# Polysketch attention in front of a SwiGLU block: late batches' queries sketched with tokens on the partitions, their denominators and turning on VectorE, numerators in 16 tiles, and the first batch reordered

## The chip, the cores and the metric

One core of one Trainium2 chip. The metric is the device time of one execution in microseconds. All runs were in the fast state (granted TensorE clock 0.995 to 1.00). Every ratio below is the mean time of one kernel's fast runs over that of the kernel before in the same rounds on the same chip, so it is not quite the ratio of the medians that stand beside it.

## The reference, cut to what matters

```python
# 4 batches, 4 heads, 1088 tokens, head size 32, sketch size r = 8
def phi(x):                                   # 64 features of a token and head
    a = einsum('rd,bhsd->bhsr', S1, x)
    b = einsum('rd,bhsd->bhsr', S2, x)
    return einsum('bhsi,bhsj->bhsij', a, b).reshape(..., r * r)
q_p, k_p = phi(q), phi(k)
kv  = einsum('bhsf,bhsd->bhfd', k_p, v)
z   = sum(k_p, axis=2)
num = einsum('bhsf,bhfd->bhsd', q_p, kv)
den = einsum('bhsf,bhf->bhs', q_p, z)[..., None] + 1e-06
x   = (num / den), heads side by side         # 4352 tokens x 128
out = (silu(x @ w_gate) * (x @ w_val)) @ w_out   # d_ff = 1536
```

The feed-forward part is most of the arithmetic: 12 blocks of tokens (384, 384 and 320 columns in each batch), 12 chunks of d_ff, three matmuls each, so 432 full-array fp32 matmuls. The weights, S1 and S2 come as 64-bit doubles and are converted on the chip; q, k and v come as fp32.

## The kernel before: the parts concerned

A *unit* is one block and one chunk: two matmuls, Silu on ScalarE, the product on VectorE. A third matmul ("down") follows. Attention for batch b+1 is a generator, advanced between units of batch b, so its work on the other engines hides behind feed-forward matmuls, and its own matmuls are *inserted* between them.

```python
def unit(i, j, late=False):
    g, u = bank(), bank()
    for o, w in ((g, wg), (u, wv)):
        nc.tensor.matmul(o[:, 0:n], w[:, j, :], xT[:, t0 : t0 + n], ...)
    nc.scalar.activation(sg, g, AF.Silu)
    nc.vector.tensor_tensor(out=hj, in0=sg, in1=u, op=ALU.mult)     # some go to GpSimd, "late"

def narrow(dst, raw, shape):          # a weight piece, 64-bit to fp32, in three stages
    nc.vector.tensor_scalar(e, hi, 0x7FF00000, ...)                 # 1: exponent, mantissa
    nc.vector.tensor_scalar(m, hi, 0xFFFFF, 0x100000, ...)
    yield
    nc.scalar.activation(e, e, AF.Relu, ...)                        # 2
    nc.scalar.activation(f, m, AF.Copy, scale=2.0**-20)
    yield
    nc.vector.scalar_tensor_tensor(out=e, in0=hi, scalar=-(1 << 31), in1=e, ...)   # 3: the sign
    nc.vector.scalar_tensor_tensor(out=f, in0=lo, scalar=2.0**-52, in1=f, ...)     #    the low word
    mul = nc.vector if first else nc.gpsimd
    mul.tensor_tensor(out=dst, in0=f, in1=e.bitcast(FP32), op=ALU.mult)
    ...

def attention(b, prods=None):         # a late batch (cut)
    ... key sketches and features on VectorE, their sums zs on GpSimd
    key_values(kvp[:, 0, :], phk, 0, NC)                   # 36 matmuls, 128*32
    for h in range(H):
        nc.tensor.matmul(kvp[32*h : 32*h+32, 1, 0:F], ones[:], zs[:, h, :], ...)
    ... turn_kv: kv and z turned and replicated by matmuls with the identity
    for i, (x0, n) in enumerate(steps):                    # three query steps
        phq = query_features(n, query_products(x0, n, tags))   # features on the partitions
        yield
        nd = totals(n, phq, kvz, ...)       # numerators AND denominators, 16 matmuls of 64*32
        divide(b, x0, n, nd)                # turn den, 1/den, turn back, num * (1/den) into xT
        yield
```

The start handles the first batch with nothing to hide behind: warm-up matmuls, sketches, key values, numerators and denominators, then `keep_warm(3, ...)` (three 512-column bf16 matmuls that compute nothing), `divide` and the first unit.

Of the kernel before, what the change touches and what calls it, by code (L numbers as in the profile page):

```python
# [1 line left out]

# [10 lines left out]
ALU = mybir.AluOpType  # L13
PSUM = bass.MemoryType.PSUM
# [3 lines left out]
def kernel(  # L18
# [37 lines left out]
    F = R * R  # L56
# [49 lines left out]
    qld = const.tile([P, NX, Dh], FP32, name="qld")  # L106
    vld = const.tile([P, H, NC, Dh], FP32, name="vld")
    kT = const.tile([P, NC, 4, 32], FP32, name="kT")
    qT = const.tile([P, HX, 2, 32], FP32, name="qT")
# [27 lines left out]
    def load_next():  # L137
        if not coming:
            return
        name, i = coming.pop(0)  # L140
        dst, src = weights[name]
        c0, c1 = pieces[name][i]
        if name == "wo":
            part = src.rearrange("(c p) d -> p c d", p=P)[:, c0:c1, :]
        else:
            part = src.rearrange("p (c f) -> p c f", f=P)[:, c0:c1, :]
        if not wide_w:
            nc.sync.dma_start(out=dst[:, c0:c1, :], in_=part)
            return
        t = raw[name, i] = stage.tile([P, 3, P], I64, tag="raw", name="raw", bufs=NRAW)  # L150
        nc.sync.dma_start(out=t[:, 0 : c1 - c0, :], in_=part)
# [4 lines left out]
    nc.gpsimd.memset(kld[:, NX : 4 * NC, :], 0.0)  # L156
    nc.gpsimd.memset(vld[96:128, :, NC - 2 : NC, :], 0.0)
    load_k(0)
    load_q(0, 0, 2 * XS)
    for i in range(NRAW if wide_w else len(coming)):  # L160
        if i == 2:
            load_v(0, [nc.sync] * 4)
            load_q(0, 2 * XS, 4 * XS)
        load_next()
    load_q(0, 4 * XS, NX)
# [5 lines left out]
    ones = const.tile([P, Dh], FP32, name="ones")  # L171
# [29 lines left out]
    def narrow(dst, raw, shape):  # L201






        words = raw.bitcast(I32)
        pat = "p (n w) -> p n w" if len(shape) == 2 else "p c (n w) -> p c n w"
        words = words.rearrange(pat, w=2)  # L210
        lo = words[..., 0].bitcast(U32)
        hi = words[..., 1]
        first = len(shape) == 2
        tag = "s" if first else ""
        e, m = (
            stage.tile(shape, I32, tag=n + tag, name=n, bufs=6) for n in ("exp", "man")
        )
        f = m[:].bitcast(FP32)
        nc.vector.tensor_scalar(e[:], hi, 0x7FF00000, None, op0=ALU.bitwise_and)  # L219
        nc.vector.tensor_scalar(  # L220
            m[:], hi, 0xFFFFF, 0x100000, op0=ALU.bitwise_and, op1=ALU.bitwise_or
        )
        yield
        nc.scalar.activation(e[:], e[:], AF.Relu, bias=rebias[: shape[0], :], scale=8.0)  # L224
        nc.scalar.activation(f, m[:], AF.Copy, scale=2.0**-20)
        yield
        nc.vector.scalar_tensor_tensor(  # L227
            out=e[:], in0=hi, scalar=-(1 << 31), in1=e[:],
            op0=ALU.bitwise_and, op1=ALU.bitwise_or,
        )  # L230
        nc.vector.scalar_tensor_tensor(  # L231
            out=f, in0=lo, scalar=2.0**-52, in1=f, op0=ALU.mult, op1=ALU.add
        )
        mul = nc.vector if first else nc.gpsimd
        mul.tensor_tensor(out=dst, in0=f, in1=e[:].bitcast(FP32), op=ALU.mult)  # L235
        if not first:
            load_next()
        yield
# [26 lines left out]
    def turn_q(x0, n):  # L265
        nc.vector.transpose(
            out=qT[:, x0 : x0 + n, :, :].rearrange("p x a t -> p (x a) t"),
            in_=qld[:, 2 * x0 : 2 * x0 + 2 * n, :],
        )

    def key_products(ps, c0, c1):

        for c in range(c0, c1):
            for a in (0, 2):
                nc.tensor.matmul(  # L275
                    ps[32 * a : 32 * a + 64, 64 * (c - c0) : 64 * (c - c0) + 64],
                    kT[:, c, a : a + 2, :].rearrange("p a t -> p (a t)"),
# [39 lines left out]
    def unit_sums(kz, phk, c0, c1):  # L317

        for c in range(c0, c1):
# [3 lines left out]
                ones[:],  # L323
# [5 lines left out]
    def turn_kv(kvs, kzp):  # L329

        for half in range(2):
            nc.tensor.matmul(  # L332
                kzp[F * half : F * half + F, 0:P], kvs, ident[:], start=True, stop=True
            )

    def query_products(x0, n, tags):
# [3 lines left out]
        for pr in range(2):  # L340
# [8 lines left out]
            for t in range(2):  # L349
                for half in range(2):  # L350
                    for g in range(2):
# [4 lines left out]
                            qT[r, x0 : x0 + n, half, :],  # L356
# [39 lines left out]
    def totals(n, phq, kvz, nd):  # L396

        w = 32 * n
        for t in (1, 0):
# [16 lines left out]
    def divide(b, x0, n, nd, among=()):  # L416
# [10 lines left out]
        )  # L427
        nc.vector.tensor_scalar_add(rc[:, 0 : 2 * n], dT[:, 0 : 2 * n, 0], 1e-6)
# [4 lines left out]
        if among:  # L433
            part(*among)
# [13 lines left out]
        for x, num, r in todo:  # L448
            nc.vector.tensor_tensor(out=x, in0=num, in1=r, op=ALU.mult)

    def feature_sums(phk):
# [8 lines left out]
        return s[:, 0, :].rearrange("p (h f) -> p h f", h=H)  # L460

    def next_keys(tag):

        both = wide(tag)
        for i, c in enumerate(kpieces):
            key_products(both[:, i, :], *c)
        return [key_copy(both[:, i, :], *c) for i, c in enumerate(kpieces)]

    def attention(b, prods=None):


        if prods is None:
            for c in kpieces:
                turn_k(*c)
                yield
            load_k(b + 1)
            prods = next_keys("b")
        phk = apool.tile([P, NC, H, R, R], FP32, tag="phk", name="phk")
        key_features(phk, prods[0], *kpieces[0])
        yield  # L480
        key_features(phk, prods[1], *kpieces[1])
        zs = feature_sums(phk)
        yield
        kvp = wide("a")
        key_values(kvp[:, 0, :], phk, 0, NC)
        for h in range(H):
            nc.tensor.matmul(
                kvp[32 * h : 32 * h + 32, 1, 0:F], ones[:], zs[:, h, :], start=True, stop=True
            )
        kvs = apool.tile([P, 2, F], FP32, tag="kvs", name="kvs")  # L490
        nc.scalar.copy(kvs[:], kvp[:, :, 0:F])
        if b + 1 < B:
            load_v(b + 1, [nc.sync] * 4)
        turn_q(*steps[0])
        yield
        kvz = apool.tile([P, 2, P], FP32, tag="kvz", name="kvz", bufs=2)
        kzp = bank()[:, 0 : 2 * P].rearrange("p (t n) -> p t n", t=2)
        for t in range(2):
            turn_kv(kvs[:, t, :], kzp[:, t, :])
        nc.scalar.copy(kvz[:], kzp)  # L500
        kvz = kvz[:, 0, :], kvz[:, 1, :]
        tags = "ab"
        for i, (x0, n) in enumerate(steps):
            phq = query_features(n, query_products(x0, n, tags))
            if i + 1 < len(steps):
                turn_q(*steps[i + 1])
            elif b + 1 < B:
                load_q(b + 1)
                turn_k(*kpieces[1])
                if b + 2 < B:  # L510
                    load_k(b + 2)
            yield
            nd = totals(n, phq, kvz, side_by_side(tags[0]))
            last = i + 1 == len(steps)
            if last and b + 1 < B:
                prods = next_keys(tags[1])
            divide(b, x0, n, nd)
            if i == 1 and b + 1 < B:
                turn_k(*kpieces[0])
            tags = tags[::-1]  # L520
            if last:
                return prods
            yield

# [84 lines left out]
    keep_warm(18, 64)  # L609
# [6 lines left out]
    s32 = sraw  # L616
    if wide_s:
        s32 = const.tile([2 * R, Dh], FP32, name="s32")
        run(narrow(s32[:], sraw[:], [2 * R, Dh]))
# [9 lines left out]
    keep_warm(3, ps=bank("acc"))  # L629
# [31 lines left out]
    kvs, zs = (apool.tile([P, F], FP32, name=x) for x in ("kvs0", "zs0"))  # L661
    kvz = [apool.tile([P, P], FP32, name=x) for x in ("kvz0", "kvz1")]
    qbs.append(query_copy(n, *pss[1]))
    nc.scalar.copy(zq[:], kz)
    part("wg", 0)
    key_values(kv, phk, *fpieces[0])
    key_values(kv, phk, *fpieces[1])
    phq = query_features(n, pss, qbs)
    zp = bank("g2")
    for h in range(H):  # L670
        nc.tensor.matmul(
            zp[32 * h : 32 * h + 32, 0:F], sel[:], zq[:, F * h : F * h + F],
            start=True, stop=True,
        )
    key_values(kv, phk, *fpieces[2])
    nc.vector.tensor_copy(zs[:], zp[:, 0:F])
    turn_q(*steps[1])
    for t, s, to, tag in ((1, zs, None, "g0"), (0, kvs, kv, "g1")):
        if to is not None:
            nc.vector.tensor_copy(s[:], to)  # L680
        ps = bank(tag)
        turn_kv(s[:], ps)
        nc.scalar.copy(kvz[t][:], ps[:, 0:P])
    part("wv", 0)
    part("wg", 0)
    nd = totals(n, phq, kvz, ([bank(t) for t in ("g2", "acc")], side_by_side("a")[0]))
# [4 lines left out]
    divide(0, *steps[0], nd, among=("wv", 0))  # L691
# [3 lines left out]
    att = attention(1)  # L695
# [12 lines left out]
    turn_q(*steps[2])  # L708
    unit(0, 2, late=True)
    part("wg", 2)  # L710
# [8 lines left out]
    for _ in range(2):  # L719
# [12 lines left out]
    for z, p in enumerate(both(3, *w) + both(4, *w) + [("wo", i) for i in range(4)]):  # L732
        z += z // 2 * 3
        for at in (z, z + 1, z + 2):
# [5 lines left out]
    groups = (17, 19, 21, 23, 27, 29)  # L740
    for z, (i, j) in enumerate(seq):
# [5 lines left out]
        if z in (16, 24, 25, 26):  # L747
# [9 lines left out]
        if z in groups:  # L757
            next(att)
    todo.sort()
    keys = None  # L760

    def attend():

        nonlocal att, keys
        try:
            if att:
                next(att)
        except StopIteration as end:
            att, keys = None, end.value

    while todo:
# [3 lines left out]
        attend()  # L775
    while att:
        attend()
# [3 lines left out]
    groups = (0, 1, 6, 9, 12, 15, 18, 21, 24)  # L781
    for b in range(1, B):
        att = attention(b + 1, keys) if b + 1 < B else None
        for z in range(3 * NCH):
# [5 lines left out]
            if z in groups:  # L790
                attend()
        while att:
            attend()
# [42 lines left out]
```

## Time and profile before

| | before |
|---|---|
| median of three runs | 321.68 us (321.27 to 321.79) |
| profiled span | 320.2 us, clock 1.00 |
| first feed-forward matmul | 16.70 us |
| 432 feed-forward matmuls at pace | 263.3 us (0.645 us each at 384 columns, 0.538 at 320) |
| inserts and waits of TensorE | 35.8 us: 5.9 up to 52 us (first batch), 29.9 after it (batches 1 to 3) |
| tail | 4.4 us |

This is a ledger: the four parts add to the span. It is read from the timeline of TensorE: the distance between the starts of two neighbouring feed-forward matmuls, less the pace, is what the work or the wait between them costs. Busy time would mislead here, because small matmuls overlap. Starts are measured, while ends are modelled. The lines themselves stand in the prediction.

Where VectorE matters is better seen in busy times by stretch. The columns are the stretch, its length, busy microseconds (and instructions) of PE, PEld, DVE, ACT and POOL, the clock, the DMA share and GB/s. The kernel before:

```profile
17.00:40.00 23.00, 21.45 (x155) 12.09 (x154) 19.71 (x51) 15.74 (x38) 7.80 (x8) 1.00 0.46 131
40.00:60.00 20.00, 19.75 (x65) 11.66 (x63) 17.72 (x37) 10.45 (x23) 7.09 (x7) 1.00 0.47 139
```

On average over the kernel VectorE has half its time free.

### The profile page before, as it was taken

The page shows a single profiled execution, that of the slowest core. Times are in us where ns is not written, and L with a number is a line of the kernel's source. Part 1 is how long each engine was busy: PE and PEld are TensorE (multiplying, and loading weights), DVE is VectorE, ACT ScalarE, POOL GpSimd, SP SyncE. Part 2 cuts the span into 40 slices and gives each one's busy share as a digit, 9 for nine tenths or more (in the row PEclk, how much of TensorE's full clock was granted, in tenths as well). Part 3 has the DMA queues.
Part 4 walks back from the last instruction along what each step waited for, and adds up shares of the span by engine and source line. Part 5 has one row for each costly group of instructions (what it writes and reads, how often), then busy time and mean ns, then how long its engine had stood idle before and what let it go on. Part 6 is the DMA issues. An engine that isn't in the chain of part 4 may idle for free.

```text
span 320.2 us, 5609 instructions
## 1 busy us (share of the span) xinstructions
PE 311.3 (97%) x2300; PEld 193.8 (61%) x2300; DVE 156.5 (49%) x332; ACT 98.6 (31%) x227; POOL 37.7 (12%) x53
## 2 busy tenths in 40 slices
PE   8979999999999999999999999999999999999994
PEld 6545565666566555555676665555667655676664
DVE  4797999543674433555522623535443332323321
ACT  3457765222112223223222223131322222222230
POOL 2224234163000600000000410000000000000000
PEclk9999999999999999999999999999999999999999
DMA  7553490204025020120010100010010100100101
GB/s 201 160 151 100 127 279 0 72 0 97 2 35 151 0 72 2 25 73 0 5 22 0 22 2 3 6 20 0 2 25 0 21 0 2 26 0 0 21 2 25
DMA packets 24665, 13.99 MB, mean 44 GB/s; under 512 B 18368, under 2 KB 22720, under 8 KB 24640
## 3 DMA queue, kind: packets, MB, share of 16 engines
q1 hardware_dynamic: 24000, 13.54, 16.6%
q8 instruction: 18, 0.29, 0.4%
q10 hardware_dynamic: 640, 0.10, 0.2%
q14 instruction: 7, 0.06, 0.1%
HBM read 11.41 MB, written 2.23 MB: 43 GB/s over the span
## 4 chain that ended last, share of the span: by engine, by line
PE 87%; DVE 8%; issue 2%; ACT 1%; POOL 0%; DVEq 0%
PE bank L539 48%; PE bank L567 27%; DVE hj L553 2%; PE a L403 2%; PE a L353 2%; PE bank L197 1%; PE b L353 1%; PE b L275 1%; PE a L309 1%; DVE exp L227 1%; PE a L581 1%; DVE man L231 1%; PE b L403 1%; PE bank L332 1%; DVE exp L219 1%
## 5 line engine op out<-in xcount | busy, mean ns | idle before, releaser
L553 DVE TENSOR_TENSOR hj<-sg,bank 128x384 f32<-128x384 f32 (+1 forms) x138 | 72.5, 527 | 119.7 <-PE bank L539 118.9
L545 ACT ACTIVATE sg<-bank 128x384 f32<-128x384 f32 (+1 forms) x144 | 67.9, 471 | 163.9 <-PE bank L539 162.9
L539 PE MATMUL bank<-xT,wg 128*128 128x384 f32 (+1 forms) x288 | 113.4, 476 | 1.7 <-POOL wg L235 1.1
L539 PE MATMUL bank<-xT,wv 128*128 128x384 f32 (+1 forms) x288 | 111.6, 469 | 0.5 <-DVE hj L553 0.5
L567 PE MATMUL bank<-hj,wo 128*128 128x384 f32 (+2 forms) x288 | 106.9, 463 | 0.4 <-DVE hj L553 0.2
L539 PEld LDWEIGHTS bank<-xT,wv 128*128 128x128 f32 x288 | 54.5, 190 | 34.4 <-DVE hj L553 2.1
L567 PEld LDWEIGHTS bank<-hj,wo 128*128 128x128 f32 x288 | 53.8, 190 | 34.0 <-issue 1.9
L539 PEld LDWEIGHTS bank<-xT,wg 128*128 128x128 f32 x288 | 53.1, 190 | 32.7 <-issue 3.3
L455 POOL TENSOR_TENSOR zs<-phk 128x1024 f32<-128x1024 f32 x3 | 7.0, 2350 | 109.4 <-DVE phk L298 109.4
L381 DVE TENSOR_TENSOR phq<-a,qb 128x384 f32<-128x384 f32 (+1 forms) x11 | 5.8, 527 | 9.2 <-ACT qb L367 9.2
L353 PE MATMUL b<-qT,sq 32*64 32x192 f32 (+1 forms) x176 | 9.3, 324 | 0.0
L353 PE MATMUL a<-qT,sq 32*64 32x192 f32 (+1 forms) x176 | 9.2, 324 | 0.0
L224 ACT ACTIVATE exp<-exp,rebias 128x384 int32<-128x384 int32 (+3 forms) x15 | 8.2, 550 | 3.0 <-DVE exp L219 2.3
L595 DVE STREAM_TRANSPOSE o<-bank 128x384 f32<-128x384 f32 (+2 forms) x12 | 6.5, 543 | 5.4 <-PE bank L567 5.2
L227 DVE SCALAR_TENSOR_TENSOR exp<-raw,exp 128x384 int32<-128x384 int32 (+2 forms) x14 | 8.6, 618 | 0.9 <-ACT exp L224 0.9
L298 DVE TENSOR_TENSOR phk<-ka,b 128x1280 f32<-128x1280 f32 (+1 forms) x6 | 8.1, 1342 | 1.7 <-ACT ka L292 1.7
L367 ACT COPY qb<-a 128x384 f32<-128x384 f32 (+1 forms) x11 | 5.1, 460 | 11.2 <-PE a L353 5.2
L367 ACT COPY qb<-b 128x384 f32<-128x384 f32 (+1 forms) x11 | 5.1, 463 | 9.5 <-PE b L353 6.1
L424 DVE STREAM_TRANSPOSE dT<-a 128x384 f32<-128x384 f32 (+1 forms) x8 | 4.4, 550 | 7.4 <-PE a L403 7.4
L381 DVE TENSOR_TENSOR phq<-b,qb 128x384 f32<-128x384 f32 (+1 forms) x11 | 5.8, 525 | 3.9 <-ACT qb L367 3.9
L353 PEld LDWEIGHTS a<-qT,sq 32*64 32x64 f32 x176 | 5.5, 131 | 3.0 <-PE bank L539 1.6
L231 DVE SCALAR_TENSOR_TENSOR man<-raw,man 128x384 f32<-128x384 uint32 (+2 forms) x14 | 6.9, 492 | 0.0
(90 smaller groups left out, 166.4 us busy)
## 6 DMA issues: line engine op xcount, KB each, us to landing
kld<-in_k_dram SPq DMA_DIRECT2D x4, 544.0 KB, 5.0
vld<-in_v_dram SPq DMA_DIRECT2D x12, 144.0 KB, 4.3
qld<-in_q_dram SPq DMA_DIRECT2D x3, 544.0 KB, 4.4
raw<-in_moe_w_out_dram SPq DMA_DIRECT2D x4, 384.0 KB, 4.7
out_dram<-o SPq DMA_DIRECT2D x28, 48.0 KB, 1.8
raw<-in_moe_w_gate_dram SPq DMA_DIRECT2D x3, 384.0 KB, 3.2
raw<-in_moe_w_val_dram SPq DMA_DIRECT2D x3, 384.0 KB, 3.2
out_dram<-o SPq DMA_DIRECT2D x16, 40.0 KB, 1.7
```

Source lines behind the costliest of these rows:

```text
L224: nc.scalar.activation(e[:], e[:], AF.Relu, bias=rebias[: shape[0], :], scale=8.0)
L227: nc.vector.scalar_tensor_tensor(out=e[:], in0=hi, scalar=-(1 << 31), in1=e[:], op0=ALU.bitwise_and, op1=ALU.bitwise_or,)
L231: nc.vector.scalar_tensor_tensor(out=f, in0=lo, scalar=2.0**-52, in1=f, op0=ALU.mult, op1=ALU.add)
L298: engine.tensor_tensor(out=phk[:, c0:c1, :, :, :].rearrange("p c h i j -> p (c h) i j"), in0=ka.unsqueeze(3).to_broadcast([P, n, R, R]), i ...
L353: nc.tensor.matmul(parts[g][F * half : F * half + F, t, 0:w], sq[r, t, :, :].rearrange("p i j -> p (i j)"), qT[r, x0 : x0 + n, half, :], s ...
L367: nc.scalar.copy(qb[:, :, 0:w], both[:, :, 1, 0:w])
L381: nc.vector.tensor_tensor(out=phq[:, 2 * pr : 2 * pr + 2, 0:w], in0=both[:, :, 0, 0:w], in1=qb[:, :, 0:w], op=ALU.mult,)
L403: nc.tensor.matmul(halves(nd[t])[half][32 * h : 32 * h + 32, 0:w], kvz[t][r, 32 * h : 32 * h + 32], phq[r, h, 0:w], start=True, stop=True,)
L539: nc.tensor.matmul(o[:, 0:n], w[:, j, :], xT[:, t0 : t0 + n], start=True, stop=True)
L545: nc.scalar.activation(sg[:, 0:n], g[:, 0:n], AF.Silu)
L553: nc.vector.tensor_tensor(out=hj[:, 0:n], in0=sg[:, 0:n], in1=u[:, 0:n], op=ALU.mult)
L567: nc.tensor.matmul(acc[i][:, 0:n], wo[:, j, :], hidden[i, j][:, 0:n], start=(j == 0), stop=(j == NCH - 1),)
```

## The change

Its intent: take small matmuls off TensorE, the bound engine, and let VectorE do that work where it has time; and shorten the chain of latencies before the first unit. The diff cut to its core:

```diff
 def attention(b, qsteps):
+    # queries turned and sketched exactly like the keys, tokens on the partitions
+    for ps, src in ((kp, kT), (qp, qT[:].rearrange(...))):
+        for i, c in enumerate(kpieces):
+            key_products(ps[:, i, :], *c, src=src)
...
-    for h in range(H):
-        nc.tensor.matmul(kvp[32*h : 32*h+32, 1, 0:F], ones[:], zs[:, h, :], ...)
+    nc.tensor.matmul(kvz[:, 1, 0 : H * F], ones[:], zs, ...)      # one 128-wide sum
...
-    turn_kv ...
-    for i, (x0, n) in enumerate(steps):
-        phq = query_features(n, query_products(x0, n, tags))
-        nd = totals(n, phq, kvz, side_by_side(tags[0]))
-        divide(b, x0, n, nd)
+    kv turned by two 128*128 matmuls with the identity
+    for s0, s1 in qsteps:                     # batch 1: two steps; later: one
+        for c0, c1 in thirds:
+            nc.vector.tensor_tensor(out=prod, in0=zrep[...], in1=fac[...], op=ALU.mult)
+            yield
+            nc.vector.tensor_reduce(
+                out=dot[:, x, :],
+                in_=phq[:, c0:c1, :, :, :].rearrange("p c h i j -> p (c h) j i"),
+                axis=AX.X, op=ALU.add)
+            yield
+        dot *= b of the query; den = sum of dot + 1e-6; 1/den; a of the query *= 1/den
+        for c0, c1 in thirds:
+            key_features(phq, ...); yield     # features, already divided
+            nc.vector.transpose(out=phT[...], in_=phq[...]); yield
+        for g in range(2):
+            for h in range(H):
+                for a in range(4):            # 16 tiles of 32*32: row a, column h
+                    nc.tensor.matmul(num[a // 2][32*h : 32*h+32, a % 2, 0 : 32 * n],
+                        kvr[32*a : 32*a+32, g, 32*h : 32*h+32], phT[32*a : 32*a+32, h, g, s0 : s0+n, :],
+                        start=(g == 0), stop=(g == 1))
+        copies to xT, half on ScalarE, half on VectorE
...
 # the conversion of a weight piece of two chunks
-    mul.tensor_tensor(out=dst, in0=f, in1=p2, op=ALU.mult)                  # GpSimd
+    first half on VectorE, second half on GpSimd
...
 # the start
-    keep_warm(18, 64)
+    keep_warm(9, 64)
-    keep_warm(3, ps=bank("acc"))             # 512 columns each, after the sketch matrices
+    keep_warm(2, ps=ps); keep_warm(16, 32, ps=ps)
     first weight pieces loaded later and through ScalarE's queue, values before them
-    sums of features: selected by a matmul, copied, turned by matmuls, copied
+    turn_sums(zq, sel[:], ps)                 # turned directly, one copy
+    totals(n, phq, kvz, nd, which=(1,))       # denominators before the numerators
     divide: conversion steps of the second weight pieces moved between its operations
 # one operation of attention per unit where it was one group in every second or third
```

## The prediction

> **What bounds the kernel now.** I read the page first (engine shares, then the chain of waits), then the timeline of the TensorE alone, then the groups by shape for durations, and at the end the timeline of all engines for the first 40 us.
>
> ```profile
> PE 311.3 (97%) x2300; PEld 193.8 (61%) x2300; DVE 156.5 (49%) x332; ACT 98.6 (31%) x227; POOL 37.7 (12%) x53
> PE   8979999999999999999999999999999999999994
> DVE  4797999543674433555522623535443332323321
> PE 87%; DVE 8%; issue 2%; ACT 1%; POOL 0%; DVEq 0%
> ```
>
> TensorE is the bound: 97% busy, 87% of the chain that ended last. VectorE is full only in slices 4 to 6 (24 to 48 us, where the weights are converted). So I count the time as a TensorE ledger: what each piece of work pushes the next feed-forward matmul back by. One feed-forward matmul (two passes, "x2") comes every 0.645 us at 384 columns and every 0.538 us at 320; that is 0.84 ns a column and pass. In the timeline of batch 2 the attention pieces stand between such matmuls:
>
> ```profile
> 133.57 0.81 PE L567 MATMUL bank<-hj,wo 128*128 128x384 f32 x2
> 134.31 0.39 PE L353 MATMUL b<-qT,sq 32*64 32x192 f32 x4
> ...
> 135.17 0.91 PE L539 MATMUL bank<-xT,wg 128*128 128x384 f32 x2
> 135.92 0.81 PE L539 MATMUL bank<-xT,wv 128*128 128x384 f32 x2
> ...
> 140.43 0.81 PE L567 MATMUL bank<-hj,wo 128*128 128x384 f32 x2
> 141.17 0.88 PE L403 MATMUL b<-phq,kvz 64*32 64x192 f32 x32
> 141.98 0.91 PE L539 MATMUL bank<-xT,wg 128*128 128x384 f32 x2
> ...
> 187.10 0.81 PE L567 MATMUL bank<-hj,wo 128*128 128x384 f32 x2
> 187.83 1.21 PE L309 MATMUL a<-phk,vld 128*32 128x64 f32 x72
> 188.86 0.29 PE L487 MATMUL a<-zs,ones 128*32 128x64 f32 x8
> 189.09 0.91 PE L539 MATMUL bank<-xT,wg 128*128 128x384 f32 x2
> ```
>
> The reader sees that an insert costs start to start minus 0.645, plus 0.11 because the matmul behind it takes 0.75 instead of 0.645. Query sketches (32 passes): 135.17-133.57-0.645+0.11 = 1.06 us, and 0.96 at 160 columns. Numerators with denominators (L403): 1.01, 1.01 and 0.90. Key values with feature sums: 1.46, of which the 8 sum passes are 0.22. The same reading gives 1.40 for key sketches alone (36 passes, 59.34 to 61.27) and 1.21 where they follow L403, and 0.60 for turning kv (L332).
>
> The ledger of all gaps: first feed-forward matmul at 16.7; 432 of them at pace, 36 x (8 x 0.645 + 4 x 0.538) = 263.2; inserts and waits 35.8, of which 5.9 in the first batch and 29.9 in batches 1 to 3 (11.8, 9.5, 8.7; the first has about 1.2 of waits); tail 4.4. Sum 320.1, against a span of 320.2. The feed-forward and the tail are not touched; the prize is in 29.9, 5.9 and 16.7.
>
> The start, from the timeline of all engines:
>
> ```profile
> 13.98 0.58 DVE L424 STREAM_TRANSPOSE dT<-a 128x384 f32<-128x384 f32 x1 [0.69 <-PE a L403]
> 16.10 0.46 POOL L235 TENSOR_TENSOR wv<-man,exp 128x128 f32<-128x128 f32 x1 [2.27 <-DVE man L231]
> 16.70 0.88 PE L539 MATMUL bank<-xT,wg 128*128 128x384 f32 x2 [0.58 <-POOL wv L235]
> 20.33 0.91 PE L539 MATMUL bank<-xT,wg 128*128 128x384 f32 x2 [1.08 <-POOL wg L235]
> ```
>
> The first batch is one chain of latencies; TensorE waits in it, once 1.08 us for GpSimd's multiply of a weight piece.
>
> **What the Trainium skill says.** (1) "TensorE: Matmul & The Clock Gate", Part 3, Measured speedup vs the span model: small matmuls on separate 32-row and 32-column tiles run side by side, 16 of them at 10.6 times. The trace agrees for 8 tiles: 32 passes of 192 columns one by one would be 32 x 0.161 = 5.2 us; L403 costs 1.01. No run yet shows 16 tiles. (2) "TensorEngine Tiling (Array Packing)", Key Properties and Gotcha 1: changing the mode drains the engine, and row tiles need different PSUM banks. The first fits the 0.37 us that L403 costs above 4 rounds x 0.161; the new numerators put each row tile in its own bank. (3) "VectorE: DVE Perf Modes", the perf-mode tier table: fp32 tensor_tensor and tensor_reduce run at one element a cycle. The trace: tensor_tensor 936 ns at 768 elements, 1481 at 1280, so 1.06 ns an element plus 0.12 us. No reduce is in the trace; I take it like a tensor_tensor of the elements it reads.
>
> **The change part by part.** TensorE, a late batch with one query step:
> - Removed: three query sketches, 1.06 + 1.06 + 0.96 = 3.08; three numerator and denominator groups, 2.92; the feature replication kv turn, 0.60. The old key sketches (1.2 to 1.4) and key values with sums (1.46) come back changed. Together about 9.3, which with waits is the 29.9 / 3.
> - Keys and queries sketched alike, tokens on partitions: 72 passes, 1.40 + 1.21 = 2.61.
> - Key values 1.46 - 0.22, plus one 128-wide sum of 256 columns in two passes, 2 x 256 x 0.84 ns = 0.43: 1.67.
> - kv turned by two 128-column full-array matmuls: 4 x 0.108 = 0.43, say 0.5.
> - Numerators: 64 passes on 16 tiles, so 4 rounds of 288 (half of them 256) columns: 4 x 0.242 = 0.97, plus 0.37 as at L403: 1.34. Key values issue 72 passes in 1.03, 14 ns each, so 64 need at least 0.92: issue does not forbid it.
> - Sum 6.1. Batch 1 has two query steps; two small groups bounded by issue at 1.1 each make it 7.0. Three batches: 19.2.
>
> VectorE, a late batch. Before: key and query turns 3.2, key features 2.7, query features 3.2, turning and inverting denominators 4.6, final product 1.6: 15.3 us. After: turns of keys and queries 3.1; key features 2.9; products with z 3 x 0.94 and three reduces like them, 5.6; the denominator group of five small operations about 1.7; query features 2.8; their turning 3 x 0.97 = 2.9 (a 640-element turn takes 0.84); half of the final copies 0.7. Sum 19.7, 4.4 more. Between 177 and 250 us VectorE is busy 31.9 of 73.0; it would be 36 of about 70. It is not the bound on average. In detail: one attention operation per unit, at most 0.97 (1.7 for the denominator group) beside a 0.55 product, in a unit of 1.93 us (1.61 at 320 columns). A unit's second bank is wanted again 2.6 us after it is full and the product needs 0.8 of that, so a lump of 1.7 fits, nearly. I allow 1.3 us in all for waits: at changes of block, where the output turn sits behind such an operation, and around the 20 us in which weight conversion and batch 1's turns share VectorE. ScalarE loses about 0.7 us a batch; it doesn't matter.
>
> So batches 1 to 3: 29.9 -> 19.2 + 1.3 = 20.5, **9.4 less**.
>
> First batch. Half the second warm-up goes, so the sketch matmul needn't wait for it until 4.80; the keys land at 1.28 + 4.0 = 5.3 all the same, so only 0.15 is won. Denominators: the sums copy ends at 10.98 (10.8 then); turned directly, in 16 short passes, they need 0.35 + 0.3 for the copy instead of two matmul groups and two copies, and the query features are done at 11.1. So the denominators' matmuls start near 11.6 and their turn near 12.2 instead of 13.98. Then conversion steps 0.55, add, reciprocal, turn 1.0, products 0.6: xT at about 14.9 instead of 16.5; the value weights' last steps come after it, to about 15.9. First feed-forward matmul at about 15.2 instead of 16.7: **1.5 less**. The second weight pieces are multiplied half on VectorE (about 0.3) and half on GpSimd (0.46) instead of 1.18 on GpSimd: most of the 1.08 wait goes, **0.9 less**. The first weight load is issued about 1 us later from ScalarE's queue but no longer ahead of the values; it is first read at 9.2, so I expect it just in time.
>
> Sum: 9.4 + 1.5 + 0.9 = 11.8; 321.7 - 11.8 = **309.9**.
>
> **Rivals.** A: sixteen tiles don't run side by side, or drain longer. At 8 at a time each large group costs 8 x 0.242 + 0.37 = 2.3; four groups add 4 us: 313.5. For it: no 16-tile group in the trace; against it: the 8-tile groups reach all but 0.37 us of the ideal. B: VectorE takes over. From 40 to 60 us it is already busy 17.7 of 20.0, and the new schedule puts an attention operation in every unit there instead of every second; on 320-column blocks a 1.0 us operation with a 0.49 product fills 1.5 of 1.61. Late products hold banks and TensorE waits 2 to 4 us: 312 to 314. Against it: after 60 us the trace has VectorE idle 1.1 to 1.5 us in most units, and lateness can be made up. C: the start wins nothing, because weights come late through the second queue or because VectorE, 19.7 busy of 23.0 from 17 to 40 us, sets the pace again before 50 us: 312. GpSimd's sums (about 5.3 us for four operations, three to four units ahead of their use) could add tenths.
>
> **Range and chances.** A, B or C alone leaves 312 to 314; two together 316. The ledger's removed terms are measured, so the gain can hardly go below 6 us unless two rivals strike. If there are no new waits it is 308. Hence 309.9, range 306.8 to 314.0. 2% faster means under 315.2: chance 0.88; within 2% 0.11; slower 0.01.
>
> **What would show it.** Right: numerator groups of 64 passes costing about 1.3; 72 sketch passes about 2.6; VectorE near 170 us busy; first feed-forward matmul near 15.2; batches 1 to 3 costing about 20 above pace. Wrong: numerator groups above 2; waits of TensorE on the product hj or the output turn of many tenths in each unit of batches 1 to 3 (B); a long wait at the first weight conversion or a lead-in still above 16 (C); a reduce far over 0.94 us, which would feed B.

## The result, and the profile after

| | before | after |
|---|---|---|
| median, same rounds | 321.55 us (4 runs) | 311.81 us (311.34 to 312.32, 4 runs) |
| profiled span | 320.2 | 309.6 |
| first feed-forward matmul | 16.70 | 16.28 |
| feed-forward at pace | 263.3 | 263.3 |
| inserts and waits to 52 us | 5.9 | 5.4 |
| inserts and waits in batches 1 to 3 | 29.9 | 20.4 |
| tail | 4.4 | 4.2 |

The ratio is 0.970 (95%: 0.968 to 0.972), so 3% faster. The predicted 309.9 us was 1.9 us too low, with the measured time inside the range. Now the page of the kernel after, engine shares, the slices of VectorE, and the chain that ended last:

```profile
PE 302.3 (98%) x2068; PEld 191.0 (62%) x2068; DVE 176.4 (57%) x333; ACT 96.0 (31%) x228; POOL 37.2 (12%) x54
DVE  4897999752758655269944552897532323333321
PE 87%; DVE 8%; ACT 2%; DMA 1%; issue 1%; SPq 0%; DVEq 0%
```

TensorE has 232 instructions and 9 us less, VectorE 20 us more, and the bound is the same: the chain is still TensorE's for 87%. The slices of VectorE now show bumps (slices 18 to 20 and 26 to 28) where a late batch's products, features and turns stand.

The inserts of a late batch, from the timeline of TensorE (start, length, line, output and operands, array mode, shape, count):

```profile
114.53 0.81 PE L679 MATMUL bank<-hj,wo 128*128 128x384 f32 x2
115.27 1.27 PE L278 MATMUL a<-s,kT 128*64 128x64 f32 x36
116.37 1.22 PE L278 MATMUL b<-s,qT 128*64 128x64 f32 x36
117.52 0.91 PE L651 MATMUL bank<-xT,wg 128*128 128x384 f32 x2
118.27 0.81 PE L651 MATMUL bank<-xT,wv 128*128 128x384 f32 x2
...
128.59 0.81 PE L679 MATMUL bank<-hj,wo 128*128 128x384 f32 x2
129.33 1.21 PE L312 MATMUL a<-phk,vld 128*32 128x64 f32 x72
130.47 0.70 PE L528 MATMUL a<-zs,ones 128*128 128x256 f32 x2
131.00 0.81 PE L651 MATMUL bank<-xT,wg 128*128 128x384 f32 x2
131.65 0.81 PE L651 MATMUL bank<-xT,wv 128*128 128x384 f32 x2
```

```profile
155.98 0.70 PE L679 MATMUL bank<-hj,wo 128*128 128x320 f32 x2
156.61 0.43 PE L602 MATMUL a<-phT,kvr 32*32 32x288 f32 x2
156.62 0.41 PE L602 MATMUL b<-phT,kvr 32*32 32x256 f32 x2
...
157.78 0.37 PE L602 MATMUL b<-phT,kvr 32*32 32x256 f32 x1
158.11 0.81 PE L651 MATMUL bank<-xT,wg 128*128 128x320 f32 x2
```

Sketches of keys and queries: 117.52 - 114.53 - 0.645 = 2.35, and 0.11 because the matmul behind them takes 0.75 (117.52 to 118.27): 2.46 us. Key values with sums: 131.00 - 128.59 - 0.645 = 1.77; here the next distance is 0.65, the pace, so nothing is added. Numerators: 158.11 - 155.98 - 0.538 = 1.59, and 0.10 behind them: 1.69. The turn of kv costs 0.45, and batch 1's two smaller numerator groups 1.09 (96 columns) and 1.37 (192 and 160). Summed over three batches the work is 19.8 us; about 0.5 us of waits make it 20.4.

The start of the kernel after:

```profile
15.52 0.82 PE L195 MATMUL a<-const-bfloat16-1.0 128*32 128x512 bf16 x3
16.28 0.91 PE L651 MATMUL bank<-xT,wg 128*128 128x384 f32 x2
...
19.06 0.88 PE L651 MATMUL bank<-xT,wg 128*128 128x384 f32 x2 [0.25 <-DVE wg L238]
20.32 0.88 PE L651 MATMUL bank<-xT,wv 128*128 128x384 f32 x2 [0.38 <-DVE wv L238]
```

In brackets stands how long TensorE waited and for whom. The wait of 1.08 us for GpSimd's multiply is gone, but waits of 0.25 and 0.38 us for VectorE's half of that multiply have come. The three warm-up matmuls of `keep_warm` take TensorE from 15.52 until the first unit.

Against each other: batches 1 to 3 gave 9.5 us of the 10.6 between the two profiled spans, and all that the prediction had asked of them (9.4); the start gave about 1, where it had asked for 2.4. And part of that 1 is chance: the first turn of the keys, which waits for their load, began between 5.36 and 5.99 us in the traces. Up to 52 us several kernels of the next section differ in nothing but the start, so their traces can be counted together. With the old start the first feed-forward matmul came at 16.70 and 16.52 us (the kernel before and late_only); with the new one it came between 16.28 and 16.90 in seven traces (the kernel after, its repeat, first_only, num_twice, num_rows_outer, product_twice, reduce_unit_stride). The inserts and waits up to 52 us were 5.9 and 6.0 with the old start, 5.3 to 5.4 with the new one. So the new start is worth about 0.6 us: nothing at the first matmul, all of it in the inserts and waits.

### The profile page after: what moved, and what is told of

Read it like the earlier page. It is cut to its first block, busy times and chain, and to the rows that moved or that the text cites. A ratio compares the mean times of both kernels' runs of the same rounds, so it can differ in the third digit from the quotient of the medians.

```text
span 309.6 us, 5154 instructions
## 1 busy us (share of the span) xinstructions
PE 302.3 (98%) x2068; PEld 191.0 (62%) x2068; DVE 176.4 (57%) x333; ACT 96.0 (31%) x228; POOL 37.2 (12%) x54
## 4 chain that ended last, share of the span: by engine, by line
PE 87%; DVE 8%; ACT 2%; DMA 1%; issue 1%; SPq 0%; DVEq 0%
PE bank L651 50%; PE bank L679 28%; DVE hj L665 2%; DVE exp L225 1%; PE a L602 1%; DMA kld<-in_k_dram 1%; PE a L278 1%; PE a L312 1%; PE b L278 1%; DVE exp L217 1%; DVE man L229 1%; PE a L693 1%; PE a L528 1%; ACT exp L222 1%; PE bank L324 1%
## 5 line engine op out<-in xcount | busy, mean ns | idle before, releaser
L679 PE MATMUL bank<-hj,wo 128*128 128x384 f32 (+2 forms) x288 | 105.3, 460 | 0.2 <-DVE hj L665 0.2
L565 DVE TENSOR_REDUCE dot<-phq 128x96 f32<-128x768 f32 x9 | 13.8, 1532 | 0.0
L301 DVE TENSOR_TENSOR phk<-kas,a 128x512 f32<-128x512 f32 (+1 forms) x12 | 8.7, 749 | 5.2 <-ACT kas L509 5.2
L589 DVE STREAM_TRANSPOSE phT<-phq 128x768 f32<-128x768 f32 x9 | 8.7, 968 | 0.1
L301 DVE TENSOR_TENSOR phq<-qab 128x768 f32<-128x768 f32 x9 | 8.6, 951 | 0.0
L558 DVE TENSOR_TENSOR phq<-zrep,qab 128x768 f32<-128x768 f32 x9 | 8.5, 942 | 0.0
L620 ACT COPY xT<-a 128x64 f32<-128x64 f32 (+4 forms) x9 | 2.4, 332 | 15.9 <-PE b L602 9.5
L217 DVE TENSOR_SCALAR exp<-raw 128x384 int32<-128x384 int32 (+2 forms) x14 | 6.8, 486 | 0.3 <-DMA raw<-in_moe_w_val_dram 0.3
L223 ACT ACTIVATE man<-man 128x384 f32<-128x384 int32 (+3 forms) x15 | 6.8, 453 | 0.0
L263 DVE STREAM_TRANSPOSE kT<-kld 128x384 f32<-128x384 f32 (+2 forms) x9 | 6.1, 692 | 0.3 <-DMA kld<-in_k_dram 0.3
```

Source lines behind the costliest of these rows:

```text
L217: nc.vector.tensor_scalar(e[:], hi, 0x7FF00000, None, op0=ALU.bitwise_and)
L301: engine.tensor_tensor(out=phk[:, c0:c1, :, :, :].rearrange("p c h i j -> p (c h) i j"), in0=ka.unsqueeze(3).to_broadcast([P, n, R, R]), i ...
L558: nc.vector.tensor_tensor(out=prod, in0=zrep[:].unsqueeze(1).to_broadcast([P, n, H * R, R]), in1=fac.unsqueeze(3).to_broadcast([P, n, H * ...
L565: nc.vector.tensor_reduce(out=dot[:, x, :], in_=phq[:, c0:c1, :, :, :].rearrange("p c h i j -> p (c h) j i"), axis=AX.X, op=ALU.add,)
L589: nc.vector.transpose(out=phT[:, :, :, c0:c1, :].rearrange("p h g c t -> p c (h g) t"), in_=phq[:, c0:c1, :, :, :].rearrange("p c h (g i) ...
L679: nc.tensor.matmul(acc[i][:, 0:n], wo[:, j, :], hidden[i, j][:, 0:n], start=(j == 0), stop=(j == NCH - 1),)
```

## The experiments

Theory S ("VectorE sets the pace early"): the whole gain is from the late batches. The start gained nothing, because up to 52 us TensorE follows VectorE's weight conversions, and a shorter way to the first unit only makes it wait later. Rival L ("lead-in"): the start is worth what the first unit moves, and only the warm-up matmuls in the way hid it. A second set asks what the late batches' terms are made of, and how much room VectorE has left.

### The two halves by themselves

Each kernel is the one before with only the late batches' hunks, or only the start's and the conversion's hunks, of the change.

```diff
 first_only: + reordered start, loads, split multiply   (attention of late batches as before)
 late_only:  + new attention(b, qsteps) and its schedule (start, loads, multiply as before)
```

> Only the first batch reordered (loads, direct turn of the sums, split multiply, shifted conversions); later batches as before. Theory S (the start gained little because VectorE's conversions, not TensorE's lead-in, pace the kernel up to about 50 us; read from the traces: first feed-forward 16.70 to 16.28, first-batch inserts 5.87 to 5.40): 0.9 us less than before, about 320.7. The prediction on record had 2.4 less: 319.2. A third: the late part hides some of the start's gain by its extra VectorE work from 52 us on, then first_only gains 1.5 or more alone.

> Only batches 1 to 3 changed; loads and first batch as before. Theory S: the late batches carry the whole gain (ledger above pace in batches 1 to 3 from 29.9 to 20.4): 9.4 to 9.9 us less than before, about 312.0; first feed-forward matmul at 16.7 and the keys landing 4.0 us after issue, as in the kernel before. Rival: the two halves need each other (conversion steps were moved to make room for the late part's VectorE work from 52 us on), then TensorE waits between 50 and 60 us grow by 0.5 us or more and the total is above 312.8.

The start alone: 321.5 us (six runs, 320.8 to 322.7), ratio 1.000 (0.998 to 1.002). The six runs lie in two groups, three at 320.8 to 321.0 and three at 322.0 to 322.7, so the start gains about 0.7 us in one half of them and loses as much in the other; one trace of such a longer run is read at the end of the experiments. The late batches alone: 312.04, ratio 0.970 (0.969 to 0.971), the same as the whole change (a repeat of that in five rounds gave 311.74 and 0.970, 0.969 to 0.971).

> The changed kernel unaltered, so that the others of this call can be compared with it on the same chip. Expected: 311.8 us, between 311.3 and 312.3, ratio to before 0.970; first feed-forward matmul at 16.3 us.

So the halves do not need each other, the late batches carry the gain, and the start's part is not told from zero: 0 with an uncertainty of 0.6 us, where 2.4 had been predicted. The 0.6 us of the traces lies at the edge of that.

### Is it the lead-in?

The first edit takes away the three warm-up matmuls in front of the first unit; the second also starts the conversion of the second pieces earlier.

```diff
 no_fill:
-    keep_warm(3, ps=wide("a")[:, 0, :])
 early_and_no_fill: the same, and
     turn_q(*steps[1])
+    part("wg", 1)
 ...
-    for _ in range(2):
-        part("wg", 1)
-        part("wv", 1)
+    part("wg", 1)
+    part("wv", 1)
+    part("wv", 1)
```

> The changed kernel without the three 512-column warm matmuls that stand before the first feed-forward matmul in TensorE's order (15.52 to 16.28 us in its trace). Theory S: the first feed-forward matmul moves to about 15.6, but the second unit's first matmul stays at 19.0 to 19.1 because it waits for VectorE's conversion of the second gate piece; total within 0.3 us of the changed kernel. Rival L (TensorE's lead-in is on the path): the whole kernel 0.65 us shorter and the second unit at 18.4.

> As no_fill, and the first two VectorE operations on the second gate piece (0.57 us) are moved into the gap of 0.75 us in which VectorE waits at 11.9 us for the denominators. Theory S: VectorE's chain after 15.4 us is 0.5 shorter, the second unit starts near 18.5 and the kernel is 0.4 to 0.6 us shorter than the changed one. Rival L: 0.65 shorter, like no_fill, and no difference between the two. If the raw piece lands later than 11.9 us, the denominators' turn is delayed and it is slower.

The start of the kernel without the warm-up matmuls:

```profile
15.87 0.88 PE L651 MATMUL bank<-xT,wg 128*128 128x384 f32 x2
16.72 0.91 PE L651 MATMUL bank<-xT,wv 128*128 128x384 f32 x2
...
19.35 0.88 PE L651 MATMUL bank<-xT,wg 128*128 128x384 f32 x2 [0.24 <-DVE wg L238]
20.61 0.88 PE L651 MATMUL bank<-xT,wv 128*128 128x384 f32 x2 [0.38 <-DVE wv L238]
```

The keys were turned 0.29 us later in this run (5.65 against 5.36), so the times are to be taken from there. The first unit then begins at 10.22 instead of 10.92: 0.7 us earlier, as L has it. But the second unit's second matmul is at 14.96 in both, behind the same two waits for VectorE. The time was 311.73, ratio 0.969 (0.968 to 0.971): nothing gained. L is out. With the earlier conversion the second unit came at 14.56, 0.4 us earlier, and the time was 311.63, ratio 0.969 (0.968 to 0.971): still within the noise.

### Is it VectorE's conversion?

One of VectorE's four operations on each weight piece is left out, so negative weights lose their sign and the result is wrong. Nothing else changes.

```diff
 no_sign:
-    nc.vector.scalar_tensor_tensor(out=e, in0=hi, scalar=-(1 << 31), in1=e, ...)
+    if first:        # S1 and S2 only
+        nc.vector.scalar_tensor_tensor(out=e, in0=hi, scalar=-(1 << 31), in1=e, ...)
```

> Wrong result on purpose: the conversion of the weights leaves out the VectorE operation that puts the sign in (14 operations, 7.4 us of VectorE, all before 52 us). Theory S (VectorE paces the kernel up to 50 us): the second unit starts 0.5 to 0.7 us earlier relative to the keys, and the waits of 0.1 to 0.34 on hj between 34 and 52 us go: 1.3 to 1.8 us shorter than the changed kernel, about 310.2. Rival: the waits there are TensorE's own latency chain, and the kernel stays within 0.4 of 311.7.

Measured: 309.54 us, ratio 0.963 (0.961 to 0.964), so 2.2 us less than with the sign (311.74). Inserts and waits up to 52 us fell from 5.4 to 3.45 us. The busy times of the kernel after, then of this one:

```profile
17.00:40.00 23.00, 22.38 (x157) 12.22 (x156) 20.48 (x51) 15.24 (x37) 8.09 (x9) 1.00 0.46 133
40.00:60.00 20.00, 19.83 (x89) 11.56 (x90) 18.32 (x38) 9.96 (x23) 7.07 (x7) 1.00 0.48 148
```

```profile
17.00:40.00 23.00, 23.00 (x160) 13.03 (x161) 19.05 (x48) 16.64 (x41) 8.69 (x10) 1.00 0.50 144
40.00:60.00 20.00, 20.00 (x132) 13.02 (x130) 15.00 (x32) 9.89 (x23) 6.47 (x7) 1.00 0.52 153
```

With 14 operations fewer on VectorE, TensorE is full in both stretches, and the waits on hj between 30 and 52 us are gone. This half of theory S is confirmed: in this stage VectorE was the pacing engine, at 89 to 92% busy, not at 100%. One thing is not told apart: the edit also takes an operation out of each weight piece's own chain, so at the second unit, where TensorE waits for the weights themselves, a shorter chain may have helped as much as a freer VectorE.

Can it be relieved with a right result? The low word was moved to ScalarE and GpSimd for the later pieces, on top of early_and_no_fill:

```diff
 low_by_act (pieces 3 and later, and w_out):
+    nc.scalar.activation(low, lo, AF.Copy, scale=2.0**-52)           # stage 2
-    nc.vector.scalar_tensor_tensor(out=f, in0=lo, scalar=2.0**-52, in1=f, ...)
+    nc.gpsimd.tensor_tensor(out=f, in0=low, in1=f, op=ALU.add)
```

> A version meant to be faster: early_and_no_fill, and for eight of the later weight pieces the low word is converted by ScalarE and added by GpSimd instead of one VectorE operation (8 x 0.55 = 4.4 us less on VectorE between 20 and 52 us). Theory S (VectorE paces that stretch; without the sign operation 1.9 us of inserts and waits went): the waits between 34 and 52 us (0.9 us) go, 310.5 to 311.0, correct result. Rival: GpSimd (1.0 us more per piece) or ScalarE becomes what the weights wait for, then the same as the changed kernel or slower.

It was slower: 312.79, ratio 0.973 (0.972 to 0.974), 1.2 us over the kernel that it started from. From the timeline of all engines:

```profile
33.25 0.60 ACT L222 ACTIVATE exp<-exp,rebias 128x384 int32<-128x384 int32 x1
33.75 0.51 ACT L223 ACTIVATE man<-man 128x384 f32<-128x384 int32 x1
34.17 0.54 ACT L226 ACTIVATE low<-raw 128x384 f32<-128x384 uint32 x1
34.61 0.74 ACT L663 ACTIVATE sg<-bank 128x320 f32<-128x320 f32 x2
...
35.08 0.81 PE L657 MATMUL bank<-xT,wg 128*128 128x320 f32 x2 [0.29 <-ACT sg L663]
...
37.20 1.01 POOL L244 TENSOR_TENSOR wv<-man,exp 128x384 f32<-128x384 f32 x1 [0.56 <-DVE exp L228]
37.37 1.04 DVE L217 TENSOR_SCALAR exp<-raw 128x384 int32<-128x384 int32 x1
...
39.07 0.35 DVE L217 TENSOR_SCALAR exp<-raw 128x384 int32<-128x384 int32 x1
```

Two things went wrong. Three conversions in a row on ScalarE (0.60, 0.51 and 0.54 us) now stand before a Silu, and the marked waits of TensorE in this stretch, four of 0.15 to 0.34 us, are all for a Silu. And VectorE was relieved by less than the 4.4 us counted. Its operations can be drawn out while GpSimd works: one and the same operation (L217) took 1.04 us beside GpSimd's multiply and 0.35 us without it. That one was as long in the kernel it started from (0.93 to 1.00 us), but with GpSimd's additions the ten sign operations at 384 columns now took 7.3 us instead of 6.1. Relief on the count of operations was not relief in time.

### What the numerators cost

```diff
 num_twice:
-    for g in range(2):
+    for g in (0, 1, 0, 1):
 num_rows_outer:
-    for g in range(2):
-        for h in range(H):
-            for a in range(4):
+    for a in range(4):
+        for g in range(2):
+            for h in range(H):
```

> Every numerator group of the late batches is issued twice (128 passes instead of 64; same result). If the 16 tiles work side by side and 0.64 us of the 1.69 is paid once per group, the second 64 passes cost 4 x 0.242 = 0.97 to 1.05 us: group 2.7, kernel 3.4 us longer in all (two large, two small groups). Rival A (8 tiles at a time): 1.9 us more per large group. If the 0.64 belongs to the passes and not to the entry: 1.6 more per large group, 5 to 6 us in all.

> The same numerator matmuls in another order: row group outermost, so that 16 passes in a row use the same 32 rows and only four column tiles. If TensorE starts matmuls of different row groups past each other (the query sketches of the kernel before show two row pairs interleaved that stand one after the other in the program), the group stays at 1.7 us. If it goes through them in order, only 4 tiles run at a time: 16 rounds of 0.23, 3.7 us and more per large group, in all 5 to 6 us longer.

Doubled: 316.13, ratio 0.983 (0.982 to 0.985), 4.4 us more. A large group went from 1.69 to 3.06, so 64 passes more cost 1.37; at 96 columns they cost 0.72, at 192 and 160 columns 1.05. So every 64 passes cost 0.40 above the prediction's four rounds (1.37 - 0.97; at 96 columns 0.72 - 4 x 0.081 = 0.40), and what a group pays only once, going into and out of the tiled mode, is another 1.69 - 1.37 = 0.32. The sixteen tiles do run side by side: one by one, 64 passes of 288 or 256 columns would be 64 x 0.2285 = 14.6 us, 10.7 times 1.37. That is near the 10.6 that the prediction took from the Trainium skill ("TensorE: Matmul & The Clock Gate", Part 3, Measured speedup vs the span model), but only at this width: at 96 columns the same sum gives 64 x 0.081 / 0.72 = 7.2 times. What the 0.40 per 64 passes is was not found out.

With the row as the outer loop the result is the same and the time 313.7, ratio 0.976 (0.974 to 0.977), 2.0 us more. A large group now:

```profile
157.52 0.74 PE L602 MATMUL a<-phT,kvr 32*32 32x288 f32 x16
157.97 0.37 PE L602 MATMUL b<-phT,kvr 32*32 32x256 f32 x1
158.03 0.47 PE L602 MATMUL a<-phT,kvr 32*32 32x288 f32 x8
158.22 0.44 PE L602 MATMUL b<-phT,kvr 32*32 32x256 f32 x4
158.27 0.47 PE L602 MATMUL a<-phT,kvr 32*32 32x288 f32 x8
158.46 1.39 PE L602 MATMUL b<-phT,kvr 32*32 32x256 f32 x27
159.78 0.81 PE L651 MATMUL bank<-xT,wg 128*128 128x320 f32 x2
```

Output a belongs to rows 0 and 1, b to rows 2 and 3, which come later in the program; yet some of b start between those of a. Only part of the work overlaps: the group costs 2.46 instead of 1.69 us. Both expectations missed (1.7 with order of no effect, 3.7 with strict order), and what the two orders show is that here consecutive passes should go to different row groups.

### What VectorE has left

```diff
 product_twice:
+    for _ in range(2):
         nc.vector.tensor_tensor(out=prod, in0=zrep[...], in1=fac[...], op=ALU.mult)
 reduce_unit_stride (adds along the wrong axis, wrong on purpose):
-    in_=phq[...].rearrange("p c h i j -> p (c h) j i")
+    in_=phq[...].rearrange("p c h i j -> p (c h) i j")
```

> The product with z is done twice on VectorE: 2.8 us more VectorE work in each late batch (9 operations of 0.94). Theory: TensorE keeps its pace and VectorE's lag is absorbed by the slack of the banks: less than 0.6 us longer in all. Rival B (VectorE is as good as the bound here: per two units 3.9 us of TensorE against 0.94 + 1.53 + 1.1 = 3.6 of VectorE): 4.5 against 3.9 per two units, waits of TensorE on hj, and 2 us or more longer.

> Wrong result on purpose: the reduce of the product with z sums over neighbouring elements instead of every eighth one; same sizes. If the 1.53 us of the reduce (0.94 was predicted) come from the stride of eight fp32 elements in what it reads, it takes 0.9 to 1.0 now; if they come from writing one sum per eight elements, it stays at 1.5. Time: VectorE has 5 us less to do in the late batches but TensorE waited there only 0.1 to 0.4 us in all: within 0.3 us of the changed kernel (311.7).

Nine operations of 0.94 us more on VectorE: 312.83, ratio 0.973 (0.971 to 0.975), 1.0 us more. That lies between the two expectations. The late batch's stretch, and one place in it, of this kernel:

```profile
140.00:160.00 20.00, 19.59 (x126) 12.15 (x125) 17.56 (x28) 5.01 (x11) 0.00 (x0) 1.00 0.07 11
```

```profile
150.72 0.81 PE L680 MATMUL bank<-hj,wo 128*128 128x320 f32 x2 [0.41 <-DVE o L708]
```

VectorE is busy 17.6 of 20 us there, in the kernel after 16.5 of 20 with TensorE full. TensorE waits for the output turn of a finished block, which stood behind 0.95 and 0.48 us of other work on VectorE. So rival B's wait is real but lay just beyond the change: with VectorE only 1.1 us busier in this stretch, TensorE waits.

The reduce reads eight numbers that lie eight apart. The group by shape in the kernel after, then with neighbours (busy us, then mean ns):

```profile
L565 DVE TENSOR_REDUCE dot<-phq 128x96 f32<-128x768 f32 x9 | 13.8, 1532 | 0.0
```

```profile
L565 DVE TENSOR_REDUCE dot<-phq 128x96 f32<-128x768 f32 x9 | 8.5, 943 | 0.0
```

Same elements, 1532 against 943 ns. The time was 311.16, ratio 0.968 (0.966 to 0.969), 0.6 us less, though this interval and that of the kernel after (0.969 to 0.971) just touch; the delays of TensorE in batch 1 at 95 to 99 us, 0.3 us behind the reduce, are gone.

### The version that beats both

The same with a right result: the product is stored with its two inner axes swapped, so that the reduce reads neighbours; on top of early_and_no_fill.

```diff
 unit_stride_right:
-    nc.scalar.copy(zrep, kvz[...])                            # (h i) j
+    nc.scalar.copy(zrep as "(h j) i -> h i j", kvz[...])      # (h j) i
-    product as c (h i) j, reduce over "p c h i j -> p (c h) j i"
+    product as c h j i,   reduce over "p c h j i -> p (c h) j i"
```

> A version meant to be faster, correct result: early_and_no_fill, with z stored transposed and the product with z written so that the reduce reads neighbouring elements. The reduce is expected at 0.94 instead of 1.53, the product at 0.94 to 1.0 as before. If both measured effects add (0.1 for the start, 0.5 for the waits of batch 1 that went with the fast reduce): 311.1 us, ratio to before 0.967. If the product with five-dimensional operands becomes slower by as much as the reduce gains: 311.6, like early_and_no_fill.

Correct, 310.75 us (five runs, four within 0.05 us), ratio 0.966 (0.964 to 0.968). That is 1.0 us below the repeat of the kernel after (0.970, 0.969 to 0.971; the intervals do not overlap), and the best. The reduce is at 942 ns, the product still 942, and ScalarE's copy of z went from 378 to 629 ns, where it does not matter. Its profiled run was the longest of the five, 311.73. Here are the first key sketches of this trace, then those of early_and_no_fill, which has the same start:

```profile
6.05 2.19 PE L278 MATMUL bank<-s,kT 128*64 128x64 f32 x36
```

```profile
6.14 1.58 PE L278 MATMUL bank<-s,kT 128*64 128x64 f32 x36 [0.43 <-DVE kT L263]
```

The 36 passes took 2.19 us here and 1.58 in each of the other thirteen traces. The trace has the full granted clock on record only from 10.1 us on, the others from 3.5 to 5.6 us on. So TensorE itself was slow at first, and the first feed-forward matmul came 11.3 us after the first turn of the keys instead of 10.2. Runs about a microsecond longer than the rest turn up elsewhere too: two of four of the kernel after, three of six of first_only, none of five of late_only or no_fill, but also two of nine of the kernel before on this chip. Only this one was traced, so it is not shown that the others have the same cause, nor that the halved warm-up (`keep_warm(9, 64)`) makes them more frequent.

## Why the prediction was right, and where not

**The bound and the way of counting** held. The feed-forward at pace was 263.3 us in both, and every microsecond gained is in the gaps between its matmuls.

**Batches 1 to 3** (9.4 us less predicted; 9.5 in the ledger; 9.8 as late_only's median): right, and the runs show the mechanism. Terms were off in size and cancelled. Over: sketches 2.61, measured 2.46; waits 1.3 in all, measured about 0.5. Under: a large numerator group 1.34, measured 1.69; the middle one 1.1, measured 1.37; key values with sums 1.67, measured 1.77. The numerators' failed term is the fixed overhead of a group of 64 passes: taken as 0.37 from a group of 32, it is 0.72, of which 0.40 comes again with every 64 passes.

**VectorE** (about 170 us busy): measured 176.4. The failed term is the reduce, taken like a tensor_tensor of the elements it reads, 0.94 us; with its stride it took 1.53, nine times 0.59 = 5.3 us. It fed rival B a little, about 0.3 to 0.6 us, and gave the one cheap improvement.

**The start** (2.4 us less): this is where the prediction was wrong, and most of the 1.9 us between 309.9 and 311.8. Its first step, "First feed-forward matmul at about 15.2 instead of 16.7", failed: it came at 16.28 to 16.90 in the seven traces, no earlier than with the old start. From the first turn of the keys to this matmul all seven took 10.92 us, where the prediction had 15.2 - 5.3 = 9.9. It did not count three warm-up matmuls that stand in TensorE's order ahead of that matmul, 0.7 us as no_fill shows, and the denominators' turn came 0.4 us later after the keys' turn than planned (12.66 instead of 12.2 in the kernel after). But removing the warm-up matmuls did not help, so a deeper step failed: that microseconds won in the lead-in add to the sum. The second unit waited for its weights until the same time. And "most of the 1.08 wait goes, 0.9 less" counted GpSimd's wait as gone, though the multiply's half moved onto VectorE, and TensorE then waited 0.25 + 0.38 us for VectorE; 0.45 of the 1.08 is left as gain, close to the 0.6 us that the traces show for the whole start. The prediction had written this down as rival C ("sets the pace again before 50 us") and took it as one risk among three; it is what happened to most of the 2.4. first_only shows that the start alone gains nothing that can be told from zero, no_fill that an earlier first unit is worth nothing, and no_sign that VectorE's conversions set the pace up to 52 us.

**Slips in the prediction's working**, none of which decides anything: the line of slices shows VectorE full in slices 5 to 7, which is 32 to 56 us, and in slice 3, not in slices 4 to 6. Without the 1.3 us of waits its sum is 308.6, not 308. Rival A's four groups add 4 us only if the two small ones of batch 1 cost as much as the large ones, and 309.9 + 4 is 313.9, not 313.5.

**The rivals.** A fell: sixteen tiles overlap 10.7 times. B struck only for tenths of a microsecond, though product_twice shows that the next microsecond of VectorE work is paid for. C struck for most of the start's 2.4 us.

**Open.** Where the 0.40 us per 64 numerator passes comes from. Why some runs are a microsecond longer: a late full clock is seen in the one that was traced. And whether the start's 0.6 us outlast that: the first turn of the keys began at 5.47 and 5.77 us in the two traces with the old order of loads, and between 5.36 and 5.99 in the twelve with the new one, so the loads show no difference, but the times of first_only do not show the 0.6 us.

## What to carry to other kernels

Price a change by what it adds between the starts of the bound engine's regular work, and check the result in the same ledger: removing small matmuls from a full TensorE onto an engine that was more than half idle in that stage paid in full. Before shortening a lead-in, ask which engine sets the pace of the stage after it, and look at the busy shares there: here TensorE waited at VectorE's pace with VectorE 88 to 92% busy, and a first unit 0.7 us earlier gained nothing. When work is moved to an engine, look at how it reads memory (stride) and in which order passes are issued; here the stride was worth about 0.6 us and the order of the passes 2.0 us, as much together as the whole reordered start had been meant to give.

## What the Trainium skill lacked or had wrong

- "VectorE: DVE Perf Modes", the perf-mode tier table, gives tensor_reduce only as 1x, without the stride. Here 768 fp32 elements a partition took 1532 ns when the reduced elements lay eight apart, and 943 ns when they were neighbours. This is a gap of that table, on which the prediction leaned, and not of the whole skill: other pages of it do treat the step between the elements that VectorE reads.
- "TensorE: Matmul & The Clock Gate", Part 3, The mechanism, says that matmuls start in program order. In the trace with rows outermost, passes into b (rows 2 and 3) start at 157.97 us, before passes into a (rows 0 and 1) at 158.03, which come earlier in the program. The page does not say either what the order of issue over tiles is worth: 2.46 against 1.69 us for the same 64 passes.
- "TensorEngine Tiling (Array Packing)", Key Properties, says that changing the mode drains the engine, but not what that costs. Here the full-array matmul behind a tiled insert took 0.75 instead of 0.645 us to the next start, and none of that (0.65) where the insert ended in a full-array matmul; a group of 64 tiled passes pays 0.32 us in all for coming and going.
